# Attention and a routed mixture of experts on one core: later places for the routing, scalar row sums, and a first unit that is turned further ahead

## The chip, the cores and the metric

The kernel runs on one core of a Trainium2 chip. The metric is the device time of one execution in microseconds (us). The core has TensorE for matmuls (PE in the rows), which also loads the weights of each matmul (PEld), VectorE (DVE), ScalarE (ACT), GpSimd (POOL), SyncE (SP), which here mainly issues transfers, and 16 DMA engines. [...]

## What is computed

Attention over 8 batches and 12 heads (448 positions, head size 64), with scores capped by a tanh, and after it a mixture of experts over the 3584 tokens of 768 numbers:

```
scores = cap * tanh(scale * q @ k.T / cap);  attn = softmax(scores);  x = attn @ v
logits = x @ w_gate                          # 3584 x 8
for idx in argsort(-logits.flatten()):       # greedy, largest logit first
    tok, e = idx // 8, idx % 8
    if assigned[tok] >= 0 or counts[e] >= 448: continue
    assigned[tok] = e;  counts[e] += 1
out[mask_e] = relu(x[mask_e] @ w1[e]) @ w2[e]   # w1[e]: 768 x 1024, w2[e]: 1024 x 768
```

Each of the 8 experts takes exactly 448 tokens. The greedy assignment falls into 8 phases: in each one the first expert that becomes full is found, with the logit at which it does, and its tokens are fixed.

## The kernel before

**Attention** takes the first 350 us. At its end come the logits of the last batch. The attention output x, transposed, is turned back by TensorE (L37), scaled by POOL (L45) and written to a table `xs` in DRAM in "units"; those of the last four batches are left for the time in which the first routing runs.

**A routing phase** (class `Routing`) finds a threshold in three searches A, B and C of 5, 6 and 5 steps. A step compares all candidates with three trial values (two comparisons on VectorE, `cmpD` at L450, one on ScalarE, `cmpA`), sums the counts with a small matmul (L454, `psR<-r_cd,r_bo`), and forms the next trial values (`fl` L458, `r_HA`, `r_HB` or `r_HC` L461). Before the searches `propose` builds the candidates (L401 to L418), TensorE turns them (`flip`, L428), VectorE copies them (`VAt`, `q`, `VBCt`). After them `best` adds rows `R` by matmuls in fp32 with a matrix of ones (L509). `finalise` then marks the tokens (`gt` L530, a scan L534), adds up places with two small matmuls (L540, L541), builds one-hot tables (`oj`, `oh`, `rj`, to L555) and makes the list of 448 row numbers with 8 matmuls (L560) and one more (L567, `psR<-ev,r_sel`, called **sel** below).

**The experts.** Each expert works on its 448 tokens in fp32 that is split in two parts (h and l). Its rows are gathered from `xs` by four indirect transfers that POOL issues (L691) into one buffer `xg`, and turned chunk by chunk (6 chunks of 128 columns, 4 transposes each, `xtr`, L700). Layer 1 has 8 units of 18 matmuls (L721, tiles of 448 columns), layer 2 has 8 tiles of 24 or 16 matmuls (L748, 384 columns), 176 in all, so an expert is 320 matmuls. Weights arrive in `w1r` and `w2r`, issued by SP once the expert's number `ei` is known, early in `finalise`; ScalarE and POOL split them (L664, L668).

**What sets the order.** From the first expert on all compute engines keep the order in which the code is written. The routing of the next expert is a Python generator. `tick()` is called after each matmul of the experts and advances the generator when as many matmuls have gone by as its last `yield` said: the table `HA`, `HB` and constants such as 4, 12, 18. So the place of a phase in the matmuls is the sum of its yields, and the next phase starts as soon as one is over. The chunks of the next expert are turned at fixed places, the first one behind matmul 260 of an expert. The gather is issued behind `sel`. The first routing has no expert to run beside; its order is written by hand for TensorE and ScalarE, with the units of x put between the counts (`UN`), and VectorE's is left to a scheduler.

## Time and profile before

| | |
|---|---|
| median of 3 runs | 959.45 us (958.63 to 960.04) |
| the profiled execution | 957.35 us, of it 955.6 us from its first to its last instruction |
| PE busy | 898.8 us (94%) |
| DVE, ACT, POOL busy | 582.9, 576.1, 348.7 us |
| mean granted clock | 0.98 |

The profiled execution lies 2.1 us below the median of the runs. Its stages by the trace: attention to about 350 us, the first routing and the first gather to about 412 us (the "seam"), the experts to 948 us, then the last rows on their way out. A time is read as microseconds from the first instruction. A row of the timeline gives the start and the length of a run of like instructions on one engine, and in brackets how long the engine sat idle before it and what ended that.

### The profile page before, as it was taken

How to read it: one execution, taken by the hardware profiler on the slowest of the kernel's cores; microseconds unless marked ns; L12 is line 12 of the kernel's file. 1: busy time of each engine (PE TensorE's matmuls, PEld its weight loads, DVE VectorE, ACT ScalarE, POOL GpSimd, SP SyncE). 2: the span in 40 equal slices, each digit the busy share in tenths (PEclk: the TensorE clock that was granted, in tenths of full speed). 3: DMA queues.
4: the chain of work that ended last, by engine and by line, in shares of the span. 5: the costliest groups of instructions: out<-in, count | busy, mean ns of one | idle time of the engine just before them, and what ended most of it. 6: DMA issues, size and time to landing. Idle time of an engine off the chain costs nothing.

```text
span 955.6 us, 16304 instructions
## 1 busy us (share of the span) xinstructions
PE 898.8 (94%) x5742; PEld 617.0 (65%) x5742; DVE 582.9 (61%) x1956; ACT 576.1 (60%) x795; POOL 348.7 (36%) x474
## 2 busy tenths in 40 slices
PE   5899999999999977599999999999999999999996
PEld 1223333333322325378889889889889889899996
DVE  3779797988879767666665556556556556211210
ACT  6999899999999937264372372462561651432520
POOL 5100000000000007473484483393492672682831
PEclk9999999999999997699999999999999999999999
DMA  9799988778872025741632624615416407551301
GB/s 128 106 139 132 172 129 163 107 149 153 167 155 47 1 116 167 242 147 37 237 108 86 226 70 126 214 42 190 160 31 223 148 11 239 182 182 51 107 9 50
DMA packets 290803, 123.01 MB, mean 129 GB/s; under 512 B 224768, under 2 KB 275712, under 8 KB 290208
## 3 DMA queue, kind: packets, MB, share of 16 engines
q1 hardware_dynamic: 282960, 91.45, 43.1%
q0 software_dynamic: 5904, 30.28, 9.0%
q8 instruction: 45, 0.74, 0.3%
q10 hardware_dynamic: 1856, 0.23, 0.2%
q14 instruction: 38, 0.31, 0.1%
HBM read 97.15 MB, written 24.77 MB: 128 GB/s over the span
## 4 chain that ended last, share of the span: by engine, by line
PE 39%; issue 6%; DMA 6%; POOL 5%; DVE 1%; ACT 0%; POOLq 0%
PE psH L721 21%; PE psH L748 15%; DMA xg<-xs,idx 6%; POOL xg L691 2%; PE psX L700 2%; POOL out_dram L733 1%; POOL w1l L668 1%; PE psR L560 1%; POOL w2l L668 1%; DVE cmpD L450 0%; PE psR L509 0%; DVE hh L728 0%; ACT hh L726 0%; PE psR L454 0%; POOL gap L666 0%
## 5 line engine op out<-in xcount | busy, mean ns | idle before, releaser
L748 PE MATMUL psH<-w2h,hh 128*128 128x384 f32 x896 | 249.2, 344 | 0.0
L748 PE MATMUL psH<-w2l,hh 128*128 128x384 f32 x512 | 175.0, 342 | 0.0
L150 ACT ACTIVATE e<-psS,s 128x896 f32<-128x896 f32 x168 | 161.1, 1001 | 20.4 <-PE psS L144 10.6
L748 PEld LDWEIGHTS psH<-w2h,hh 128*128 128x128 f32 x896 | 163.0, 189 | 0.3
L154 ACT ACTIVATE e<-e,bias,capt 128x1792 f32<-128x1792 f32 (+2 forms) x74 | 154.4, 2087 | 2.5
L721 PE MATMUL psH<-xgh,w1l 128*128 128x448 f32 x384 | 142.1, 370 | 1.5 <-POOL gap L666 1.5
L721 PE MATMUL psH<-xgl,w1h 128*128 128x448 f32 x384 | 142.7, 372 | 0.2 <-DVE xgl L703 0.2
L721 PE MATMUL psH<-xgh,w1h 128*128 128x448 f32 x384 | 142.7, 372 | 0.0
L144 PE MATMUL psS<-tq,tk 64*64 64x448 f32 x1152 | 127.4, 556 | 10.2 <-DVE rcap L229 6.7
L668 POOL TENSOR_TENSOR w1l<-w1r,w1h 128x768 fp32r<-128x768 f32 x62 | 114.2, 1841 | 30.7 <-ACT w1h L664 24.9
L668 POOL TENSOR_TENSOR w2l<-w2r,w2h 128x768 fp32r<-128x768 f32 x64 | 118.1, 1845 | 16.6 <-ACT w2h L664 12.6
L172 PE MATMUL psA<-e,nv 128*64 128x448 f32 x576 | 124.1, 552 | 0.0
L754 ACT ACTIVATE on<-psH 128x384 f32<-128x384 f32 x48 | 23.7, 493 | 134.2 <-PE psH L748 113.7
L728 DVE SCALAR_TENSOR_TENSOR hh<-psH,hh 128x64 fp32r<-128x64 f32 (+1 forms) x128 | 44.1, 386 | 97.0 <-ACT hh L726 90.6
L158 DVE TENSOR_TENSOR es<-es,e 128x896 f32<-128x896 f32 (+1 forms) x94 | 102.0, 1085 | 1.9
L748 PEld LDWEIGHTS psH<-w2l,hh 128*128 128x128 f32 x512 | 96.7, 189 | 0.0
L144 PEld LDWEIGHTS psS<-tq,tk 64*64 64x64 f32 x1152 | 36.8, 133 | 81.9 <-issue 50.9
L172 PEld LDWEIGHTS psA<-e,nv 128*64 128x64 f32 x576 | 34.9, 136 | 83.8 <-issue 70.8
L721 PEld LDWEIGHTS psH<-xgh,w1l 128*128 128x128 f32 x384 | 72.6, 189 | 7.3 <-POOL gap L666 1.9
L721 PEld LDWEIGHTS psH<-xgl,w1h 128*128 128x128 f32 x384 | 72.7, 189 | 6.1 <-DVE xgl L703 1.3
L721 PEld LDWEIGHTS psH<-xgh,w1h 128*128 128x128 f32 x384 | 72.7, 189 | 5.3 <-ACT xgh L702 0.6
L733 POOL DMA_INDIRECT out_dram<-on,idx x31 | 30.4, 981 | 118.4 <-PE psX L700 47.1
(246 smaller groups left out, 1209.2 us busy)
## 6 DMA issues: line engine op xcount, KB each, us to landing
w1r<-in_moe_w_dram SPq DMA_DIRECT2D x64, 384.0 KB
w2r<-in_moe_w_dram SPq DMA_DIRECT2D x32, 768.0 KB
k<-in_k_dram SPq DMA_DIRECT2D x92, 112.0 KB
q<-in_q_dram SPq DMA_DIRECT2D x92, 112.0 KB
nv<-in_v_dram SPq DMA_DIRECT2D x72, 128.0 KB
xs<-xn POOLq DMA_DIRECT2D x4, 1344.0 KB
xs<-xn SPq DMA_DIRECT2D x4, 896.0 KB
xd<-xT POOLq DMA_DIRECT2D x2, 1344.0 KB
```

What stands on the lines that cost most here:

```text
L144: for c in range(2): nc.tensor.matmul(ps[c*64:c*64+64,h,:S],tks[g,0][hp,o,u*128+c*64:u*128+c*64+64],tks[g,1][hp,o,:],start=True,stop=True)
L150: nc.scalar.activation(ev(g,r),ps[:,:,:S],AF.Tanh,scale=s1)
L154: nc.scalar.activation(e,e,AF.Exp,scale=capt,bias=bias)
L158: t=es_t[g]; add=lambda o,a,b: nc.vector.tensor_tensor(o,a,b,op=ALU.add)
L172: nc.tensor.matmul(avp[g,o][h*64:h*64+64,:S],z[:,j,HG*h+o,:],ev(g,3*o+j)[:,h,:],start=(j==0),stop=(o==1 and j==2 and op is None))
L668: (eng or nc.gpsimd).tensor_tensor(view(l),r,view(h).bitcast(F32),op=ALU.subtract)
L691: g=nc.gpsimd.indirect_dma_start(out=t[:n,j*DM:(j+1)*DM],out_offset=None,in_=xs,in_offset=bass.IndirectOffsetOnAxis(ap=res[p][0][:n,j:j+1] ...
L721: nc.tensor.matmul(ps[:,:C],a[:,c,:],b[:,c,:],start=(m==0),stop=(m==DC*3-1)); m+=1
L728: nc.vector.scalar_tensor_tensor(h[:,d:d+b-a],ps[:,a:b],0.0,h[:,a:b].bitcast(F32),op0=ALU.max,op1=ALU.subtract)
L733: st=nc.gpsimd.indirect_dma_start(out=dst,out_offset=bass.IndirectOffsetOnAxis(ap=ix,axis=0),in_=src,in_offset=None)
L748: nc.tensor.matmul(ps[:,:HD],h[:,f,a:a+128],spl[p,2,hf,f//2][w][:,f%2,:],start=(m==0),stop=(m==nm-1))
L754: if t<3: nc.scalar.activation(ons[p][0][:,t*DM+hf*HD:t*DM+hf*HD+HD],ps[:,:HD],AF.Copy)
```

## The change

- **Places.** The yields of a search step go from 6 and 11 (phase 1, phases from 2) to 7 and 10, and with the 3 of `HB` from 9 and 14 matmuls per step to 10 and 13. The first unit starts the generator after 18 matmuls and not 6. For phases from 2 on, `finalise` waits for matmul 145 of the expert, so for the second layer.
- **Sums.** The three rows of `best` are first added as scalars (128x1) on VectorE, so `best` has one matmul where it had two.
- **Proposals.** `propose` is cut in two: for phase 1 and the last four chunks of the logits the second half (VB, VC, K1, K2) runs behind the first comparisons.
- **Seam.** VectorE's order is now written by hand, too. Ten small matmuls on the identity stand ahead of the turn of VA, others around the matmuls of `finalise`, in place of 16 matmuls of 512 columns on `oh`.
- **First unit.** Four chunks of the first expert are turned ahead of its first matmul, two of them into buffers of the matmul results, the others inside the unit. The weight loads that wait for the gather now wait for its last piece in `xg` and not for its row numbers. The split of the second layer's weights starts one unit later for the first expert.

```
-        HA=[6,11]; HB=3
+        HA=[7,10]; HB=3
...
-                s.propose(L,0,s.NC)
+                (s.propose_a if p==1 else s.propose)(L,0,s.NC)
                 yield 30
             yield from (s.search(wp,turned if p==0 else ()) if p<s.E-1 else s.last(wp))
-            yield 4
+            yield -((p-1)*320+145) if p>1 else 4
             yield from s.finalise(wp,L,p<s.E-1)
...
-        hint[0]=next(gen,0)
+        h=next(gen,0)
+        hint[0]=max(-h-now[0],4) if h<0 else h
...
+        def total(a,b):
+            t=wp.tile([128,1],F32,name="tot",bufs=4); jk=wp.tile([128,1],F32,name="jk",bufs=2)
+            v.tensor_scalar(jk,a,b,None,op0=ALU.add,op1=ALU.add,accum_out=t)
+            return t
+        def row(a,b):
+            th=total(a,b)
             r=wp.tile([128,8],F32,name="R",bufs=6); jk=wp.tile([128,1],F32,name="jk",bufs=2)
             v.tensor_scalar(r,s.e8,th,None,op0=ALU.mult,op1=ALU.add,accum_out=jk)
...
-        yield from s.select(wp,s.V["q"],"B",[lambda: row(tA)])
+        yield from s.select(wp,s.V["q"],"B",[lambda: keep.append(total(tA,s.zero))])
...
-        mid=[lambda: row(tB)]
+        mid=[lambda: row(keep[0],tB)]
...
-        for n,r in enumerate(((s.R[0],s.R[1]),(s.R[-1],s.e8k))[a]): nc.tensor.matmul(ps[:112,0:8],s.onesf,r,start=n==0,stop=n==1)
+        nc.tensor.matmul(ps[:112,0:8],s.onesf,s.R[a],start=True,stop=True)
...
-    N0=1; UN=[2,1,2,1,0,2,2,1,2,2,0,2,2,2,2,0]
+    N0=1; UN=[1,2,1,2,0,2,2,1,2,2,0,2,2,2,0,0]
...
-    with tc.manual_schedule(engines={ET.PE,ET.Activation}):
+    with tc.manual_schedule(engines={ET.PE,ET.Activation,ET.DVE}):
...
+            for _ in range(n): nc.tensor.matmul(wu[0][:,:128],ident,ident,start=True,stop=True)
...
-        if gate: nc.gpsimd.tensor_copy(t[0:1,0,0:1],res[p][0][0:1,0:1])
+        if gate is not None: nc.gpsimd.tensor_copy(t[0:1,0,0:1],gate)
...
+        seq=[(c,k) for c in range(DC) for k in range(3)]
+        if p==0 and f==0:
+            seq=[(0,0),(0,2)]
+            for c in range(1,DC): seq+=[(c,0),(c,2),(c-1,1)]
+            seq+=[(DC-1,1)]
...
+            if p==0 and f==0 and k==1 and c<2: xtr(0,c+4)
...
-    for _ in range(16): nc.tensor.matmul(wu[:112],rt.id16,rt.oh.rearrange("p r c -> p (r c)")[:,:512],start=True,stop=True)
...
-    hint[0]=6
-    for c in range(2): xtr(0,c)
+    hint[0]=18
+    for c in range(4): xtr(0,c,ph if c>1 else None)
```

Three places of TensorE's order show what moves. The line numbers behind a plus or in "now" are those of the changed kernel, where L560, L567, L700, L721, L748 and L428 have become L577, L585, L725, L751, L778 and L435.

First the end of the first routing: `oh` and `rj` are the tables, L771 the matmuls on `oh` that fill the pause. Before, around sel:

```order
L560 LDWEIGHTS oh
L560 MATMUL psR<-rj,oh 128x56
L771 LDWEIGHTS r_id_268
L771 MATMUL psX<-oh,r_id_268 112x512
L771 LDWEIGHTS r_id_268
L771 MATMUL psX<-oh,r_id_268 112x512
L771 LDWEIGHTS r_id_268
L771 MATMUL psX<-oh,r_id_268 112x512
L567 LDWEIGHTS r_sel
L567 MATMUL psR<-ev,r_sel 128x14
```

and now:

```order
L577 LDWEIGHTS oh
L577 MATMUL psR<-rj,oh 128x56
L648 MATMUL psX<-ident 128x128 x3
L585 LDWEIGHTS r_sel
L585 MATMUL psR<-ev,r_sel 128x14
L648 MATMUL psX<-ident 128x128 x22
```

The three matmuls of 512 columns ahead of sel have become three of 128 columns; two more of 512 stood ahead of the eight L560 matmuls, and stand there no longer.

Then the first unit of the first expert. Before:

```order
L700 MATMUL psX<-ident,xg 128x128 x8
L721 MATMUL psH<-xgh,w1h 128x448
L721 MATMUL psH<-xgl,w1h 128x448
L721 MATMUL psH<-xgh,w1l 128x448
L700 MATMUL psX<-ident,xg 128x128 x4
L721 MATMUL psH<-xgh,w1h 128x448
L721 MATMUL psH<-xgl,w1h 128x448
L721 MATMUL psH<-xgh,w1l 128x448
L700 MATMUL psX<-ident,xg 128x128 x4
```

and now:

```order
L725 MATMUL psX<-ident,xg 128x128 x8
L725 MATMUL psH<-ident,xg 128x128 x8
L751 MATMUL psH<-xgh,w1h 128x448
L751 MATMUL psH<-xgh,w1l 128x448
L751 MATMUL psH<-xgh,w1h 128x448
L751 MATMUL psH<-xgh,w1l 128x448
L751 MATMUL psH<-xgl,w1h 128x448
L725 MATMUL psX<-ident,xg 128x128 x4
```

Sixteen transposes, not eight, stand ahead of the first matmul, and the matmul that needs the second part `xgl` of a chunk comes three or four places behind the chunk's first.

Last the place in the first expert where the first chunk of the second expert is turned (L700, now L725, behind matmul 260). Before:

```order
L428 LDWEIGHTS r_VC
L428 MATMUL psV<-r_id_268,r_VC 128x112
L748 MATMUL psH<-w2h,hh 128x384 x2
L748 MATMUL psH<-w2l,hh 128x384
L748 MATMUL psH<-w2h,hh 128x384
L700 MATMUL psX<-ident,xg 128x128 x4
```

and now:

```order
L778 MATMUL psH<-w2h,hh 128x384
L725 MATMUL psX<-ident,xg 128x128 x4
L778 MATMUL psH<-w2h,hh 128x384
L778 MATMUL psH<-w2l,hh 128x384
L778 MATMUL psH<-w2h,hh 128x384 x2
L778 MATMUL psH<-w2l,hh 128x384
L778 MATMUL psH<-w2h,hh 128x384 x2
L778 MATMUL psH<-w2l,hh 128x384
L435 LDWEIGHTS r_VA
L435 MATMUL psR<-r_id_270,r_VA 128x112
```

The routing has moved back against the transposes: the next phase's turns of VA and VC stood ahead of them and now VA's come behind. Counted over the whole order, sel stands behind matmul 200, 199, 198, 197, 196, 195 of experts 0 to 5 before (that of the last expert's list behind 277 of expert 5), and now behind 228, 211, 194 and, from expert 3 on, 179, that of the last list behind 179 of expert 6. The transposes of the next expert stay behind matmuls 260, 284, 292, 300, 308 and 316.

## Rows read from the trace of the kernel before

**Rows 1.** Busy time by stretch: length, busy us (instructions) per engine, clock, DMA.

```profile
355.00:372.00 17.00, 12.25 (x59) 10.09 (x60) 11.97 (x81) 11.33 (x30) 10.62 (x11) 0.50 0.48 173
399.60:406.00 6.40, 4.64 (x16) 3.23 (x17) 3.67 (x10) 1.82 (x3) 0.83 (x1) 0.50 0.95 302
410.00:956.00 546.00, 526.20 (x2967) 482.93 (x2965) 259.43 (x1293) 234.61 (x485) 295.84 (x323) 1.00 0.38 123
```

**Rows 2.** Waits of TensorE, whole run: us in total, times, longest.

```profile
PE psR L454 <- DVE cmpD L450: 10.5, 12, 2.0
PE psX L700 <- DMA xg<-xs,idx: 7.0, 11, 1.6
PE psH L721 <- POOL gap L666: 1.5, 1, 1.5
```

**Rows 3.** Timeline of TensorE at the gather for expert 1.

```profile
454.77 0.18 PE L567 MATMUL psR<-ev,r_sel 128*128 128x14 f16 x1
...
465.82 0.38 PE L700 MATMUL psX<-ident,xg 128*128 128x128 f32 x2
...
467.86 0.42 PE L748 MATMUL psH<-w2h,hh 128*128 128x384 f32 x1
```

**Rows 4.** Stretches of the first chunk's transposes, experts 2 to 5; last a later chunk.

```profile
602.97:604.91 1.94, 0.79 (x5) 0.36 (x4) 0.04 (x2) 0.47 (x2) 1.10 (x2) 1.00 0.44 145
671.43:673.16 1.73, 0.79 (x5) 0.36 (x4) 0.00 (x0) 0.35 (x1) 1.10 (x2) 1.00 0.10 34
739.75:741.06 1.31, 0.79 (x5) 0.36 (x4) 0.00 (x0) 0.17 (x1) 0.86 (x1) 1.00 0.07 26
807.21:809.05 1.84, 0.78 (x5) 0.36 (x4) 1.41 (x5) 0.00 (x0) 1.22 (x2) 1.00 0.08 30
541.00:541.36 0.36, 0.36 (x6) 0.36 (x4) 0.32 (x4) 0.00 (x0) 0.22 (x1) 1.00 0.40 117
```

**Rows 5.** Timeline of VectorE in search A of the first routing.

```profile
362.44 0.16 DVE L458 SCALAR_TENSOR_TENSOR fl<-psR,r_HA 128x4 f32<-128x4 f32 x1 [0.57 <-PE psR L454]
...
363.98 0.16 DVE L458 SCALAR_TENSOR_TENSOR fl<-psR,r_HA 128x4 f32<-128x4 f32 x1 [0.28 <-PE psR L454]
...
364.61 0.21 DVE L483 TENSOR_SCALAR_CACHE_REDUCE R<-r_e,th 128x8 f32<-128x8 f32 x1
```

**Rows 6.** Lines L505 and L530: ns min/median/max, first and last start.

```profile
L505 DVE SCALAR_TENSOR_TENSOR sx<-wt,wB,r_e8c x7: 226/227/806, 385.1 to 788.5; 112x8 f32<-112x8 f32 x7
L530 DVE TENSOR_SCALAR gt<-qq,wB x8: 235/238/1090, 385.8 to 803.8; 112x32 f32<-112x32 f32 x8
```

**Rows 7.** Timeline of POOL in the seam.

```profile
380.79 6.08 POOL L45 TENSOR_TENSOR xn<-raw,rin 112x512 f32<-112x512 f32 x6 [0.43 <-ACT raw L42]
391.50 0.73 POOL L685 MEMSET xg<- 64x768 f32 x1 [4.63 <-DMA xs<-xn]
```

**Rows 8.** Timeline of VectorE, end of the first routing.

```profile
389.69 0.39 DVE L555 TENSOR_TENSOR rj<-oj,r_idc 112x448 f16<-112x448 f16 x1
...
392.03 0.21 DVE L564 TENSOR_REDUCE ev<-ek 128x14 f16<-128x56 f16 x1
```

**Rows 9.** Timeline of TensorE, same stretch.

```profile
389.83 1.01 PE L771 MATMUL psX<-oh,r_id 112*112 112x512 f16 x2 [1.98 <-DVE oh L553]
390.63 1.04 PE L560 MATMUL psR<-rj,oh 112*128 112x56 f16 x8
...
392.75 0.22 PE L567 MATMUL psR<-ev,r_sel 128*128 128x14 f16 x1
```

**Rows 10.** Timeline of TensorE: first matmuls of the first and second unit.

```profile
403.50 0.74 PE L721 MATMUL psH<-xgh,w1h 128*128 128x448 f32 x1
...
411.86 0.37 PE L721 MATMUL psH<-xgh,w1h 128*128 128x448 f32 x1
```

**Rows 11.** Timeline of TensorE: the matmuls of `best` in expert 0.

```profile
446.25 0.66 PE L509 MATMUL psR<-R,r_onesf 128*112 128x8 f32 x6
...
446.96 0.61 PE L748 MATMUL psH<-w2h,hh 128*128 128x384 f32 x2
```

## What was predicted

> **What bounds the kernel now.** I read the busy time by stretch first. From 410 us to the end TensorE is at 1.00 and busy for 526.20 of 546.00 us [rows 1]; the experts are bound by TensorE, and only its gaps and extra matmuls can be saved there. Ahead of it lies the seam, in which a chain of counts runs between VectorE and TensorE, and in which TensorE is at 0.50 for two stretches [rows 1]: 17 us in which it is busy for 12.25, and 6.4 us in which the first unit begins. The waits of TensorE come next [rows 2]: the counts wait 10.5 us for comparisons (seam and phase 1 together), the transposes 7.0 us for gathered rows, and one unit 1.5 us for POOL. So there are three accounts: seam, gathers, routing's own matmuls. The timeline gives the price of each.
>
> **Gathers, where the change costs.** Sel for expert 1 starts at 454.77; its first transposes start at 465.82, 60 matmuls later, so 0.184 us per matmul with what lies between; experts resume at 467.86, when the last piece has landed [rows 3]. A gather thus needs 467.86-454.77=13.09 us from sel, and 60 matmuls cover 11.05 of them. That stretch is 2.04 us long, an undisturbed chunk 0.36 [rows 4], so 1.7 us are lost. For the gathers of experts 3 to 6 the same view gives 1.94-0.36=1.58, 1.37, 0.95 and 1.48 [rows 4].
>
> By the order, sel now stands behind matmul 228, 211, 194, then 179. The first gather loses 28 matmuls of its cover, 28*0.184=+5.15 us. The second loses 12: +2.2. The third gains 4: -0.7 of its 1.58. The next three gain 16 to 18, about 3 us, more than they lose: -(1.37+0.95+1.48)=-3.8. I leave the 13.09 as it is, since the weight loads that share the DMA engines are released with the expert's number, which moves with sel.
>
> TensorE will then sit still for some 6.8 us at 466 and for 4 at 534. Behind the gather of the seam, with a pause of the same kind, the first 6.4 us ran at 0.50 [rows 1], busy for 4.64, so half of that, 2.3, was lost. No row shows a fall among the experts, whose waits are under 2 us. For the first wait I take +1.9, near that row (from 0 to 3.2, half the 6.4 us at full use); for the second, shorter one, half of it, +1.0 (0 to 1.9).
>
> At expert 6 the gather for expert 7 now comes behind matmul 179 and no longer at the start of layer 1, ahead of the split of w1. The wait for POOL's `gap` [rows 2] has no cause left: -1.5, and with the restart -1.7.
>
> **Routing among the experts.** `best` holds TensorE from 446.25 to 446.96, 0.71 us for its four fp32 matmuls [rows 11]. Two go, in six phases: -6*0.355=-2.1. The scalar sums that replace them stand on VectorE, which is busy for 259 of the 546 us [rows 1]; without that cover each would cost about the 0.21 of `R` [rows 5]. From expert 3 on the routing rests until matmul 145, which costs nothing as long as the gather keeps its cover: 260-179=81 matmuls, 14.9 us against 13.09. The later split of w2 for expert 0 costs nothing either: its last pieces, cut in unit 7, are needed 88 matmuls into layer 2. In phase 1 steps come every 10 matmuls, which is 0.2 us more per step for a chain that is late at 9; against it, the second half of the proposal and the first unit's work are put on VectorE ahead of a count. I take +0.3, from -1.5 to +1.5: neither half of the seam's and phase 1's 10.5 us [rows 2] is separable in advance.
>
> **The seam.** Its end is set by the chain from the first comparison to the list of rows.
> (a) In search A and B three counts stand behind eight transposes at half clock, and `fl` then waits 0.57 where it else waits 0.28 [rows 5] (two such, and one of 0.69): 1.0 together. Ten matmuls now fill part of TensorE's pause ahead of VA's turn. If they keep the clock up, all of it goes; I take -0.6 (0 to -1.0).
> (b) `R` (0.21 us) stands ahead of the first comparisons of B and C [rows 5] and now behind them, where VectorE waits for the count anyway: -0.4.
> (c) `sx` and `gt` take 0.806 and 1.090 us in the seam against medians of 0.227 and 0.238 [rows 6], both at 385 us, under POOL's products, which run from 380.79 to 386.87 [rows 7]. By the table `UN` the two units behind the fifteenth step have moved ahead, so POOL should be done: -(0.58+0.85)=-1.43, from 0.
> [...]
> (d) `rj` is done at 390.08 [rows 8]; the L560 matmuls start at 390.63, behind two of 512 columns [rows 9]: -0.45. `ev` is done at 392.24 [rows 8], sel starts at 392.75 behind three more [rows 9]: -0.3, as three short ones remain.
> (e) Costs: sel's matmul of `best` waits for one more sum. No row has a sum of 128x1; the nearest, `R` of 128x8, takes 0.21 [rows 5]. Less the dropped matmul: +0.2. The second half of the last proposal moves from over VA's turn to over the first count; VectorE then waits for the longer of the two: +0.2.
> [...]
> Sum of the chain: -0.6-0.4-1.43-0.75+0.4=-2.8.
>
> **First gather and unit.** The weight loads now wait for the last gathered piece, not for the numbers: -0.2, an estimate between 0 and -1. The first unit runs from 403.50 to 411.86 [rows 10], 8.36 us. Eighteen matmuls of 448 columns at 0.184*448/384=0.21 and four chunks of transposes at 0.36 [rows 4] make 5.3; of the 3.1 over, 2.3 are the clock of [rows 1], and 0.8 are waits for `xgl` and for transposes in between. The new order spreads these and starts with eight transposes more, during which the clock can rise: -1.1 (0 to -2.2, if also half the clock's cost goes).
>
> **Sum.** +5.15+1.9+2.2+1.0-0.7-3.8-1.7 = +4.05 for the gathers; -2.1+0.3 for the routing; -2.8 for the chain; -0.2-1.1 for the first unit: -1.85. On the profiled execution's 957.35 that is 955.5; it lies 2.1 under the median of the runs, 959.45, and the forecast is on that: **957.6 us**.
>
> **Rivals.**
> *The clock stays low after the first late gather* (slower). If it needs, after 7 us of stillness, what it needed in the stretch of 17 us, in which TensorE was busy for 12.25 at 0.50 [rows 1], the loss is 6.1 and not 1.9: 957.6+4.2=961.8. It decides from about 3.8 us over my 2.9, so from 13 us of matmuls at half clock in the two places together. For it: the same clock did fall after short pauses in the seam. Against: behind a gather it lasted only 6.4 us.
> *The seam gives nothing* (the same). If the products of POOL still meet `sx` and `gt`, (c) is 0; if the gather's last piece sets when the first unit can run, and the memset of `xg`, which waits for the last units' writing to `xs` and ends at 392.23 [rows 7], sets when the gather starts, the rest of the gain goes too: 957.6+1.43+1.3=960.3, within 0.2% of before. For it: that memset ends under 2 us ahead of the list. Against: the units end sooner now.
> *The seam gives more* (faster). The ten matmuls hold the clock, so all of (a); the first unit saves 2.2, phase 1 0.5 and the first late gather ends at full clock: 957.6-0.4-1.1-0.8-1.9=953.4.
> *The late gathers do not bite* (the change does less than its order says). If a gather that starts later meets fewer loads and lands 5 us sooner after sel, the +5.15, +2.2, +2.9 go: 957.6-10.25=947.3. For it: 13.09 us is long against the 403.50-392.75=10.75 us from sel to the first matmul in the seam [rows 9, 10]. Against: the stretches of the later gathers [rows 4] stay between 1.3 and 1.9 us, with other loads beside each (DMA share 0.07 to 0.44).
>
> **Chances and range.** Forecast 0.42 (its own range 955.5 to 960), clock stays low 0.15, seam nothing 0.20, seam more 0.18, no bite 0.05. About 1.9 us, 0.2%, is what a measurement of this kernel can tell from no change. The forecast lies at that edge, so half of its 0.42 is faster and half the same; with the two fast rivals that makes 0.44 faster, 0.41 the same, 0.15 slower. The range leaves out the last rival and the ends of the next two: 951.5 to 962.5.
>
> **What would show it.** Right: TensorE waits for `xg` twice, near 467 for 6 to 7 us and near 535 for 4, and a granted clock of 0.50 for some us behind at least the first; no such wait from expert 3 on, nor one for `gap`; the list's sel in the seam near 390 and not 392.75; `sx` and `gt` near their medians in the seam; the second unit's first matmul near 407.5 and not 411.86. Wrong: a gather that lands within 10 us of sel, a clock of 1.00 behind the waits, or a first unit that still takes 8 us. What would spoil the sum most is the price of the first late gather, the largest term on either side, since nothing of before shows a gather that late.

## The result: 0.3% slower

The changed kernel takes 961.91 us (median of 18 runs, 960.0 to 963.92), the kernel before 958.56 (18 runs, 957.44 to 960.7): a ratio of 1.0034, with a 95% interval of 1.0026 to 1.0041. That is 3.3 us more, where 1.85 less was forecast. More runs put the median of before 0.9 us under the one the forecast was made on; its time of 957.6 would be 956.7 on the new base. The range held the time, the sign was wrong.

The two profiled executions lie 5.7 us apart (963.07 and 957.35), 2.4 more than the medians. Part of this is the seam, whose end moves by about 1 us from one execution to the next: four kernels of this study that have the gather and the first unit of before (sums_alone, sums_padded, sums_in_place, places_alone) reach the first expert matmul at 404.3 to 404.9 us, the kernel before in its profile at 403.5. One issue of the first gather on POOL makes 0.9 us of that: it took 1.18 us in the profile of before and 2.05 to 2.07 in those four.

A ledger by stages, from the starts of instructions in the two timelines, shows where the 5.7 us lie:

| stage | before, us | after, us | difference |
|---|---|---|---|
| up to VA's turn | 354.22 | 353.78 | -0.4 |
| VA's turn to the last count of the first routing | 29.16 | 33.00 | +3.8 |
| last count to sel | 9.37 | 7.76 | -1.6 |
| sel to the first expert matmul | 10.75 | 13.34 | +2.6 |
| first unit | 8.36 | 5.03 | -3.3 |
| second unit to layer 2 of expert 0 | 30.44 | 32.43 | +2.0 |
| layer 2 of expert 0 (gather for expert 1) | 38.78 | 45.84 | +7.1 |
| expert 1 (gather for expert 2) | 68.66 | 71.42 | +2.8 |
| experts 2 to 5 | 273.17 | 265.57 | -7.6 |
| experts 6 and 7, to the last matmul | 124.20 | 124.67 | +0.5 |

The waits of TensorE over the whole run (us in total, times, longest) answer to [rows 2]; the wait for POOL's `gap` is gone, the one for gathered rows has grown from 7.0 to 11.0:

```profile
PE psR L461 <- DVE cmpD L457: 11.7, 11, 2.7
PE psX L725 <- DMA xg<-xs,idx: 11.0, 10, 2.1
```

TensorE's timeline at the gather for expert 1 answers to [rows 3]:

```profile
462.71 0.18 PE L585 MATMUL psR<-ev,r_sel 128*128 128x14 f16 x1
...
470.70 0.33 PE L725 MATMUL psX<-ident,xg 128*128 128x128 f32 x1 [2.15 <-DMA xg<-xs,idx]
...
475.37 0.67 PE L778 MATMUL psH<-w2h,hh 128*128 128x384 f32 x1
```

The experts resume 475.37-462.71=12.66 us behind sel (13.09 before), and 32 matmuls cover 5.84 of it (470.70 less the 2.15 of idle time, from sel). The matmuls that follow are slow: 0.67 against 0.42 in [rows 3]. The busy time by stretch (length, busy us of each engine, clock, DMA), for the two low stretches of the first routing and behind the two late gathers, answers to [rows 1]:

```profile
357.60:364.40 6.80, 4.96 (x24) 4.15 (x25) 5.16 (x38) 4.64 (x13) 4.05 (x4) 0.50 0.46 147
...
367.80:398.50 30.70, 22.90 (x113) 20.16 (x112) 20.71 (x120) 15.64 (x37) 18.77 (x18) 0.50 0.61 182
...
475.40:480.60 5.20, 5.20 (x19) 4.89 (x20) 1.84 (x6) 1.88 (x4) 1.82 (x1) 0.51 0.08 26
...
548.70:552.10 3.40, 3.40 (x16) 3.40 (x16) 1.30 (x9) 1.33 (x3) 1.29 (x1) 0.50 0.02 5
```

TensorE stands still, then works 5.2 us at a granted clock of 0.51, where 1.00 is full speed. About half of them, 2.6, is lost, an estimate from that clock; the 384-column matmuls start every 0.32 us there, and behind the same gather before every 0.17. Behind the second late gather the clock is low, 0.50, for 3.4 us, from 1.2 us after the experts resume (547.48). In the first routing it is low, 0.50, for 6.8 and for 30.7 us, where it was for 17 [rows 1] and for 10.2:

```profile
385.70:395.90 10.20, 6.33 (x24) 3.68 (x24) 6.97 (x29) 0.86 (x2) 3.73 (x5) 0.50 0.91 258
```

This, too, changes from one execution to the next: p1_whole, which leaves the first routing as the change has it, is low there for 13.7 and 17.0 us.

The row that was not expected is in VectorE's timeline. The second half of phase 1's proposal stands behind the first two comparisons:

```profile
412.93 1.47 DVE L418 TENSOR_SCALAR r_b<-r_u 112x32 int32<-112x32 int32 x1
...
414.65 1.95 DVE L420 TENSOR_TENSOR r_VB<-r_P,r_Bt 112x256 f16<-112x256 f16 x1
```

POOL at the same time, and the count that waits:

```profile
412.49 1.85 POOL L693 TENSOR_TENSOR w1l<-w1r,w1h 128x768 fp32r<-128x768 f32 x1 [6.86 <-issue]
414.27 0.09 POOL L691 MEMSET gap<- 1x1 f32 x1
414.47 1.85 POOL L693 TENSOR_TENSOR w1l<-w1r,w1h 128x768 fp32r<-128x768 f32 x1
```

```profile
419.30 0.19 PE L461 MATMUL psR<-r_cd,r_bo 128*128 128x4 bf16 x1 [2.65 <-DVE cmpD L457]
```

One op ends at 414.40, POOL's split at 414.34; the next long one at 416.60, POOL's next split at 416.32. An op is called held below if it is longer than its like elsewhere and ends thus, at the end of what POOL runs or shortly behind it. Right behind the wait of 2.65 us the clock falls as well:

```profile
419.00:422.40 3.40, 3.10 (x9) 2.80 (x10) 2.06 (x12) 3.23 (x8) 2.31 (x3) 0.50 0.89 229
```

By line (count: ns min/median/max) these ops in the changed kernel and, second fence, in the kernel before:

```profile
L418 DVE TENSOR_SCALAR r_b<-r_u x15: 160/166/1473, 95.2 to 806.2; 112x4 int32<-112x4 int32 x8, 112x32 int32<-112x32 int32 x7
...
L420 DVE TENSOR_TENSOR r_VB<-r_P,r_Bt x15: 192/424/1952, 95.6 to 806.6; 112x32 f16<-112x32 f16 x8, 112x256 f16<-112x256 f16 x7
...
L457 DVE TENSOR_SCALAR_CACHE_REDUCE cmpD<-r_qt,th x63: 426/442/446, 367.7 to 785.5; 128x224 bf16<-128x224 f16 x63
```

```profile
L411 DVE TENSOR_SCALAR r_b<-r_u x15: 160/165/178, 95.6 to 800.9; 112x4 int32<-112x4 int32 x8, 112x32 int32<-112x32 int32 x7
...
L413 DVE TENSOR_TENSOR r_VB<-r_P,r_Bt x15: 191/194/428, 96.0 to 801.3; 112x32 f16<-112x32 f16 x8, 112x256 f16<-112x256 f16 x7
```

Before, no op of the proposal was ever held: none began while POOL ran a split or a product. The comparisons never are held, though 139 of the 224 in the changed kernel began while POOL ran one (447 ns at most). So there are ops on VectorE that wait for POOL and ops that don't, and the change moved the eight ops of the second half from where POOL was quiet to where it is busy; two of them were held in phase 1.

In the seam the same happens to the second half of the last proposal. VectorE, and POOL's two products beside it:

```profile
355.70 0.92 DVE L420 TENSOR_TENSOR r_VB<-r_P,r_Bt 112x32 f16<-112x32 f16 x1
...
356.73 0.90 DVE L422 TENSOR_SCALAR r_Ct<-r_c 112x4 f16<-112x4 int32 x1
```

```profile
355.51 2.09 POOL L45 TENSOR_TENSOR xn<-raw,rin 112x512 f32<-112x512 f32 x2 [3.38 <-ACT raw L42]
```

The two ops end at 356.62 and 357.63, the second just behind POOL's two products (357.60).

### The profile page after: what moved, and what is told of

Its sections match the earlier page's. It is cut to its first block, busy times and chain, and to the rows that moved or that the text cites. A ratio compares the mean times of both kernels' runs of the same rounds, so it can differ in the third digit from the quotient of the medians.

```text
span 961.3 us, 16399 instructions
## 1 busy us (share of the span) xinstructions
PE 907.7 (94%) x5776; PEld 631.6 (66%) x5776; DVE 589.7 (61%) x1984; ACT 575.5 (60%) x795; POOL 349.0 (36%) x475
## 4 chain that ended last, share of the span: by engine, by line
PE 76%; issue 8%; ACT 4%; POOL 4%; DVE 4%; DMA 3%; ACTq 0%; POOLq 0%; DVEq 0%
PE psH L751 21%; PE psH L778 19%; PE psA L172 11%; PE psS L144 10%; PE psM L191 3%; DMA xg<-xs,idx 3%; ACT e L150 3%; PE psS L149 2%; PE psX L725 2%; PE psA L179 2%; PE psL L37 2%; POOL xg L716 1%; PE psM L37 1%; ACT e L154 1%; DVE cmpD L457 1%
## 5 line engine op out<-in xcount | busy, mean ns | idle before, releaser
L778 PE MATMUL psH<-w2h,hh 128*128 128x384 f32 x896 | 252.4, 347 | 0.0
L778 PE MATMUL psH<-w2l,hh 128*128 128x384 f32 x512 | 176.4, 345 | 0.0
L778 PEld LDWEIGHTS psH<-w2h,hh 128*128 128x128 f32 x896 | 165.7, 192 | 0.2
L751 PE MATMUL psH<-xgh,w1h 128*128 128x448 f32 x384 | 143.5, 374 | 0.0
L751 PE MATMUL psH<-xgh,w1l 128*128 128x448 f32 x384 | 143.3, 373 | 0.0
L751 PE MATMUL psH<-xgl,w1h 128*128 128x448 f32 x384 | 142.5, 372 | 0.0
L693 POOL TENSOR_TENSOR w2l<-w2r,w2h 128x768 fp32r<-128x768 f32 x64 | 117.9, 1842 | 17.0 <-ACT w2h L689 13.3
L778 PEld LDWEIGHTS psH<-w2l,hh 128*128 128x128 f32 x512 | 98.0, 191 | 0.0
L751 PEld LDWEIGHTS psH<-xgh,w1h 128*128 128x128 f32 x384 | 73.2, 191 | 5.4
L751 PEld LDWEIGHTS psH<-xgh,w1l 128*128 128x128 f32 x384 | 73.1, 190 | 5.5
L751 PEld LDWEIGHTS psH<-xgl,w1h 128*128 128x128 f32 x384 | 72.9, 190 | 5.4
L756 ACT ACTIVATE hh<-psH 128x448 fp32r<-128x448 f32 x64 | 34.8, 543 | 67.1 <-PE psH L751 62.7
```

Of the source, the lines that this page charges most:

```text
L693: (eng or nc.gpsimd).tensor_tensor(view(l),r,view(h).bitcast(F32),op=ALU.subtract)
L751: nc.tensor.matmul(ps[:,:C],a[:,c,:],b[:,c,:],start=(m==0),stop=(m==DC*3-1)); m+=1
L756: nc.scalar.activation(h[:,:C],ps[:,:C],AF.Relu)
L778: nc.tensor.matmul(ps[:,:HD],h[:,f,a:a+128],spl[p,2,hf,f//2][w][:,f%2,:],start=(m==0),stop=(m==nm-1))
```

## Experiments

**Theory A**: the second half of the two proposals (phase 1, and the last chunks in the seam) is slow where it now stands, since VectorE waits there for POOL's running instruction, and this spoils a gain that is otherwise about as forecast. **Rivals**: the late places cost it all (the gathers, or the count's place in the first unit); the low clock lengthens the seam whatever the proposals do. The kernels of the experiments were timed in 4 to 12 runs each beside the kernel before on the same chip; the chip was not the same for all, so two of them are compared by their ratios to before, and microseconds of a difference come from these:

| kernel | median, us | ratio to before, 95% interval |
|---|---|---|
| changed kernel | 961.91 | 1.0034, 1.0026 to 1.0041 |
| p1_whole | 957.63 | 0.9996, 0.9987 to 1.0005 |
| seam_whole | 959.27 | 1.0016, 1.0006 to 1.0025 |
| late_quiet | 960.59 | 1.0019, 1.0010 to 1.0028 |
| places_alone | 962.55 | 1.0047, 1.0034 to 1.0059 |
| unit_alone | 957.50 | 0.9987, 0.9978 to 0.9996 |
| sums_alone | 959.19 | 1.0008, 0.9999 to 1.0017 |
| sums_padded | 959.37 | 1.0009, 0.9998 to 1.0020 |
| sums_in_place | 958.12 | 0.9993, 0.9984 to 1.0002 |
| early_whole | 945.51 | 0.9868, 0.9853 to 0.9882 |
| turn_later | 946.02 | 0.9872, 0.9857 to 0.9887 |
| issue_free | 945.18 | 0.9855, 0.9836 to 0.9873 |
| combined | 940.08 | 0.9812, 0.9796 to 0.9828 |
| combined_issue | 939.43 | 0.9801, 0.9785 to 0.9816 |
| combined_in_place | 938.28 | 0.9785, 0.9766 to 0.9803 |
| without_ten | 939.75 | 0.9795, 0.9775 to 0.9814 |

**p1_whole**, on the changed kernel:

```
-            if post and i==(2 if s.cur==1 else 0): post()
+            if post and i==0: post()
...
-            if s.cur==1: late=[lambda: s.propose_b(0,s.NC)]
...
-                (s.propose_a if p==1 else s.propose)(L,0,s.NC)
+                s.propose(L,0,s.NC)
```

> The changed kernel with the whole proposal of phase 1 ahead of its first comparisons, as before. Theory A (the second half of the proposal is slow because it now stands beside POOL's split of w1, and the first count waits for it): the wait of 2.65 us at the count near 419 goes or falls under 0.7, two ops that took 1.47 and 1.95 us fall to about 0.2 and 0.4, and the time is 2 to 2.5 us under the changed kernel, so about 1 us over the kernel before. Rival B (the first count of phase 1 is late because of its new place in the matmuls): the wait stays near 2.6 and the time with it, 3.4 us over before.

0.38% of the time goes, 3.6 us, more than theory A's 2.5; the wait of 2.65 us at that count is 0.24, and from its first matmul to layer 2 expert 0 takes 33.35 us and not 37.46. Rival B is out. The stretch in the changed kernel and, second fence, in p1_whole shows what the extra is:

```profile
407.88:445.34 37.46, 34.41 (x170) 28.97 (x169) 25.67 (x124) 22.65 (x49) 26.02 (x27) 0.94 0.40 130
```

```profile
406.69:440.04 33.35, 32.74 (x170) 27.50 (x169) 21.42 (x116) 22.67 (x49) 26.06 (x27) 1.00 0.45 145
```

TensorE stands still for 0.61 us and not 3.05, so 2.4 less, and the 3.4 us at a clock of 0.50 behind the wait, worth up to 1.7 as an estimate from that clock, are gone. What the turns of VB and VC add, which also go back to the first count, is not separated.

**seam_whole**, on the changed kernel:

```
-            first=late[0]; late[0]=lambda: (s.propose_b(s.NC-4,s.NC),first())
...
-            (r.propose if b<7 else r.propose_a)(L1,4*b,4*b+4)
+            r.propose(L1,4*b,4*b+4)
```

> The changed kernel with the whole proposal of the last four chunks ahead of VA's turn, as before; the ten matmuls on the identity stay. Theory A: the two ops of 0.92 and 0.90 us beside POOL's products go, the first two counts stand 1.9 and not 2.7 us apart, TensorE's pause of 2.2 us ahead of VB's turn goes, and the time is 0.8 to 1.5 us under the changed kernel, more if the clock then falls for a shorter time. Rival C (the seam is longer only because the clock is low for longer, whatever the proposal does): less than 0.4 us.

0.18% goes, 1.7 us. The first two counts stand at 356.37 and 357.90, 1.53 apart and not 2.67, and sel at 390.78 and not 394.54. Rival C falls as the cause of the whole; but the clock may take part: the fifteen steps from the first count to the sixteenth take 26.65 us, 1.78 each and not 1.53, and the granted clock from 358 to 386 us is between 0.53 and 1.00 in stretches of 4 us. That it makes them slower is not shown. A single trace can't price the seam: from the first count to the sixteenth it is 30.05 us in the changed kernel and 28.13 in p1_whole, which has the same seam, and 26.65 here. The price taken is that of the medians.

**late_quiet** leaves all of the change and moves POOL's split only:

```
+    split1(0,2)
     hint[0]=18
...
-            if f+2<FC: work[17 if p==0 and f==0 else 3]=[lambda: split1(p,f+2)]
+            if f+2<FC and (p or f): work[17 if p==0 and f==0 else 3]=[lambda: split1(p,f+2)]
```

> The changed kernel, all of it, but POOL's split of the third w1 piece is written ahead of the first transposes, while POOL waits for the gather, and not behind the first unit's 17th matmul. So the second half of phase 1's proposal keeps its late place, and POOL is quiet there at first. Theory A (VectorE's ops wait for POOL's running instruction): the op of 1.47 us falls to about 0.2, at most one op still waits for the next split, the wait of 2.65 us at the second count falls under 1, and the time is 1.5 to 2.5 us under the changed kernel. Rival E (eight full-width ops ahead of the second count are too many, POOL or not): the wait stays over 2 us and the time within 0.7 of the changed kernel.

VectorE's timeline has the same ops at the same place, POOL quiet up to 414.68:

```profile
413.11 0.17 DVE L418 TENSOR_SCALAR r_b<-r_u 112x32 int32<-112x32 int32 x1
...
413.54 0.42 DVE L420 TENSOR_TENSOR r_VB<-r_P,r_Bt 112x256 f16<-112x256 f16 x1
...
414.75 1.84 DVE L425 SCALAR_TENSOR_TENSOR r_K<-r_kk,r_Ct 112x32 f32<-112x32 f16 x1
```

```profile
414.68 1.85 POOL L693 TENSOR_TENSOR w1l<-w1r,w1h 128x768 fp32r<-128x768 f32 x1 [6.97 <-ACT w1h L689]
```

The two long ops are back to 0.17 and 0.42. The last op of the eight, 0.18 us long in other phases, starts 0.07 after POOL's next split and ends with it. That shows what theory A says: same place, same ops, and the length follows POOL. Rival E falls by the wait, 1.43 us and not over 2. The time falls by 0.15%, 1.4 us, a little under what theory A expected, and the two intervals overlap slightly; one op is still caught, and the count waits more than the 1 us that was expected.

**places_alone**, on the kernel before: `HA=[7,10]`, the lock to matmul 145 and `hint[0]=18` from the change, nothing else.

> The kernel before with the new places alone: 10 and 13 matmuls per step, the lock to matmul 145, the generator's start after 18. The account of the gathers by the trace of the changed kernel: +5.2 and +3.1 us for the first two, with the low clock behind them, -0.9, -1.3, -0.9 and -1.5 for the next four, -1.3 for POOL's wait: about +2.4, and with fewer stalls in phase 1 some +1.5 to +2.5 us over before. Rival D (all of the loss lies in the seam, and the places pay for themselves): no more than +0.5.

0.47%, 4.5 us, more than expected. From the first transposes' place to the next matmul the gathers for experts 1 and 2 take 7.84 and 4.28 us (2.05 and 2.18 before), and from there to the end of the expert 15.5 and 14.9 us, where before had 13.2 and 13.3. The expectation had left out the wait of the first gather's first piece. Against that, from the second unit to layer 2 expert 0 takes 28.64 us and not 30.44. Rival D is out: by themselves the places lose. Whether they lose more than the whole change the intervals don't tell.

**unit_alone**, on the kernel before: the new order of the first unit, its four chunks ahead, the gate on the last gathered piece and the later split of w2.

> The kernel before with the first unit's new order alone: four chunks turned ahead of its first matmul, the weight loads gated by the gather's last piece, the later split of w2; sel and all places as before. By the two traces the first unit takes 5.0 us from its first matmul and not 8.4, and what lies between the rows' landing and that matmul grows by 0.9: -2.4, so about 956. If it was the higher clock from the longer run of small matmuls that made the unit short and not its order: -1 or less.

0.13% goes, 1.2 us, half of what was expected, and near the -1.3 of the prediction; it lies between the theory and its rival and doesn't decide between order and clock. The first matmul comes 2.23 us later and layer 2 only 0.22 later.

**sums_alone**, on the kernel before: `total`, `row` and the single matmul of `best` from the change.

> The kernel before with the scalar sums alone, so one matmul in best where there were two. By the prediction's price, 0.355 us for each of six routings among the experts: -2.1, and about 0 in the seam: 956 to 957. If VectorE's longer chain ahead of best eats it, within 0.5 of before.

Nothing is gained (0.08% more, the interval holds 0). From layer 2 to the first transposes experts 1 to 4 each take 0.35 to 0.4 us less, as priced. But layer 1 takes 0.2 more in each of them, and 0.57 in expert 7, in which no routing runs. Layer 1 of expert 7 (start, end; 145 or 146 matmuls), in the changed kernel, in sums_alone and in sums_in_place:

```profile
892.42:922.17 29.75, 29.75 (x146) 27.04 (x146) 6.00 (x16) 14.60 (x23) 27.00 (x31) 1.00 0.16 47
```

```profile
888.53:918.28 29.75, 29.75 (x145) 27.04 (x145) 6.00 (x16) 14.61 (x23) 27.05 (x31) 1.00 0.16 48
```

```profile
887.36:916.54 29.18, 29.18 (x145) 27.05 (x145) 6.00 (x16) 14.61 (x23) 27.05 (x31) 1.00 0.16 49
```

At one clock the same 144 matmuls take 0.2066 us each or 0.2027.

**sums_padded**, the same with wider small tiles (`[128,4]` for k8s and zero, `[128,8]` for tot).

> The kernel before with the scalar sums alone, as in the run of the sums alone, but the new small tiles are as wide as what they replace: k8s and zero 16 bytes each where e8k had 32, tot 32 bytes per buffer and not 4. In the run of the sums alone each matmul of layer 1 in expert 7 took 0.2066 us and not 0.2027, and those of experts 1 to 5 0.2038 and not 0.2022. Theory F (the small tiles shift what lies behind them in memory, and an operand of layer 1 then starts in a worse place): the pitch goes back to 0.2027 and the time to 956.5, 2 us under before. Rival G (the pitch comes from something else in the routing): pitch and time stay, 959.

The same time and pitch, 0.2066 us. By the author's count from the code this edit leaves the operands of layer 1 where they are in sums_alone, so that it would not part theory from rival; the 160 bytes of the next expectation are from that count, too. No trace shows an address.

**sums_in_place** is meant to put them back (its edit against sums_alone):

```
-        s.k8s=t("k8s",[128,1])
+        kz=t("kz",[128,8]); s.k8s=kz[:,0:1]
...
-        s.zero=t("zero",[128,1]); nc.gpsimd.memset(s.zero,0.0)
+        s.zero=kz[:,1:2]; nc.gpsimd.memset(s.zero,0.0)
...
-            r=wp.tile([128,8],F32,name="R",bufs=6); jk=wp.tile([128,1],F32,name="jk",bufs=2)
+            r=wp.tile([128,8],F32,name="R",bufs=2); jk=wp.tile([128,1],F32,name="jk",bufs=2)
```

> The kernel before with the scalar sums alone, and with two buffers of R and not six and the small constants in one tile, so that weights, tokens and results lie at the addresses of the kernel before (in the run of the sums alone 160 bytes further). Theory F (the place of the layer-1 operands sets the pitch): 0.2027 us per matmul in expert 7, and the time falls by the 0.36 us per routing that best shows: 956.7, 2 us under before. Rival G (the pitch comes from another part of the sums): 0.2066 and about 959.

The pitch is 0.2027 again, and layer 1 of experts 1 to 5 takes what it took before. That is the pitch that theory F expected: what differs from sums_alone is the number of `R`'s buffers and the tile of the two constants, and no routing uses them in expert 7. That the place of the operands makes the pitch is the author's reading, and which operand it is stays open. The 2 us that were expected don't come: the time is 0.07% under before, and its interval still holds 0: from the first expert matmul on, its profiled execution is 1.0 us faster than before, although layer 1 of expert 0 is 0.8 slower; the seam ended 1.1 later.

**early_whole**, on the changed kernel: both proposals whole, `HA=[6,10]`, `hint[0]=6`, so sel behind 200 and 183.

> The changed kernel with both proposals whole and with phase 1 as early as before (9 matmuls per step, start after 6; phases from 2 on keep 13 and the lock), so sel for the first two experts' gathers stands behind matmul 200 and 183. By the account of the gathers, +5.2 and +3.1 go and -1.7 and the half of 2.2 come: 8 us less for the gathers; with the proposals 11 us under the changed kernel, less 1 for the stalls of phase 1 at 9 matmuls per step: 950 to 953. If the low clock and not the wait is what costs, the same; if the gather has a fixed place in time, not 13 us from sel, no more than 5 us under the changed kernel.

945.51, 1.32% under before and 4.5 us under the expected range. The waits for gathered rows fall from 11.0 to 3.1 us in total:

```profile
PE psX L723 <- DMA xg<-xs,idx: 3.1, 4, 1.9
```

Layer 2 of expert 0 takes 37.5 us and not 45.8, expert 1 66.7 and not 71.4, so 13.0 us for two gathers; the expectation had 8. It left out the first piece's own wait, 2.15 in the timeline above; both gathers also lose less than before (1.11 and 0.35 us from the transposes' place to the next matmul, 2.05 and 2.18 before).

**turn_later**, on the changed kernel: both proposals whole, sel where the change put it, but the chunks of the next expert at 284 to 320 for two experts:

```
-    CP=[[int(y) for y in x] for x in ',,,,,0,123,45'.split(',')]
+    CP=[[int(y) for y in x] for x in ',,,,,0,123,45'.split(',')]; CL=[[int(y) for y in x] for x in ',,,,,,012,34'.split(',')]
...
+            if p<2 and u==7: wk={16:[lambda: xtr(p+1,5)]}
+            ffn2(p,u%4,u//4,(CL if p<2 else CP)[u],wk)
```

> The changed kernel with both proposals whole, with sel where the change put it (behind 228 and 211), and for the first two experts with the next expert's chunks turned behind matmuls 284, 292, 300, 308, 316 and 320 and not 260 to 316. If the gathers cost what their cover lacks, 56 matmuls or 10.3 us stand against 12.7 us for the first, 73 or 13.4 us for the second: about 2.4 us lost at the first, at most 1 behind it for the clock, nothing at the second. Phase 1 at 10 matmuls per step takes 3.9 us less in expert 0 than at 9 in the kernel with early phases. So 942 to 945, against 945.5 for that one. If the gather's end moves with the place of the transposes, or if the chunks turned so late hold up the next expert's first unit: 947 or more.

946.02, a little over. The gather for expert 1 then costs 1.24 us, the next nothing. Two ways to give a gather its 13 us, an earlier sel or later transposes, give times within each other's interval.

**issue_free**, on early_whole: VectorE's two splits of w1 behind the proposal.

> The kernel with whole proposals and early phase 1, with VectorE's two splits of w1 behind the proposal and no longer beside the gather's issues. In all kernels of this study in which such a split starts about 0.25 us into POOL's second issue that issue takes 2.05 us, else 1.2. Theory H (the issue waits for VectorE's instruction): the second issue takes about 1.2, the last piece lands 0.9 us sooner, and the time is 0.5 to 1 us under 945.5. Rival (the second issue is slow by its place, or the transfers set the landing): no change.

POOL's second gather issue in the changed kernel, VectorE's split beside it, and then the issue in issue_free:

```profile
396.96 2.07 POOL L716 DMA_INDIRECT xg<-xs,idx  x1 [0.30 <-issue]
```

```profile
397.21 0.95 DVE L693 TENSOR_TENSOR w1l<-w1r,w1h 128x768 fp32r<-128x768 f32 x1
```

```profile
393.05 1.20 POOL L714 DMA_INDIRECT xg<-xs,idx  x1 [0.30 <-issue]
```

Theory H is borne out on the instruction, which takes 0.9 us less without the split beside it. Over the kernels of this study the second issue took 2.05 to 2.07 us in all twelve in which a split began 0.25 us into it, and 1.19 to 1.20 in the four without one. But the kernel before has the split, 0.30 us into the issue, and the issue took 1.18; so it is not every such split, and what decides is not shown. From sel to the first expert matmul it takes 12.32 us and not the 13.09 of early_whole. The time moves by 0.13%, within both intervals.

**combined**, on the changed kernel: whole proposals, `hint[0]=6` with 10 and 13 matmuls per step, later transposes for three experts, and the padded tiles.

> The changed kernel with whole proposals, the generator's start after 6, so sel behind 216, 199 and 182 for the first three gathers, the chunks of the next expert turned from matmul 284 on in the first three experts, and the padded small tiles. 68 matmuls or 12.4 us stand against 12.7 for the first gather, so nothing is lost at any gather but 0.3: 1.3 us under the kernel that turns later, 0.5 more at the third gather, and 1.1 more if theory F holds: 943. If the chunks turned at 316 and 320 hold up the next expert, 945 or more.

940.08, 3 us better than expected. Nothing is lost at any gather among the experts. 1.6 of the 3 us are expert 0's layer 1, 32.74 us against 34.38 in turn_later: TensorE stands still for 0.26 us and not 0.64, and the mean clock is 1.00 and not 0.97, as the low stretch that ends the seam reaches 2.3 us into the layer in turn_later. So most of it is the clock of one execution. **combined_issue** adds issue_free's edit:

> The same with VectorE's splits of w1 behind the proposal. By theory H 0.5 to 1 us under the combined kernel: 942 to 942.5; by its rival the same time.

939.43, in the expected direction, within the intervals. Last the tiles put back (**combined_in_place**) and, on that, no ten matmuls ahead of VA's turn (**without_ten**):

> The combined kernel with VectorE's splits behind the proposal, and with the tiles at the addresses of the kernel before. By theory F 0.57 us less in each of experts 6 and 7 and some 0.1 to 0.2 in each other one: 1.5 to 2 us under 939.4. By rival G the same time.

> The same kernel without the ten matmuls on the identity ahead of VA's turn. If they hold up the clock, it falls at 355 as in the kernel before and not near 359, three counts then wait 0.3 to 0.4 us longer for transposes, and the run takes 0.6 to 1 us more. If they hold nothing up, within 0.3 us.

combined_in_place has the lowest median, 938.28, 2.15% under before, and layer 1 of experts 6 and 7 takes 29.19 us each and not 29.75, as theory F expected; its time is 0.16% under combined_issue, within both intervals. without_ten takes 0.1% more, which is inside its interval and at the upper end of what was expected if the ten hold up the clock; but its chain of counts is no slower (16 counts from 356.27 to 382.94, against 356.27 to 383.12 in combined_issue and 356.66 to 385.24 in combined_in_place). So the ten matmuls show no gain, and none is ruled out.

## Why the prediction was wrong

**The step that failed** is the price of the proposals' second halves. The prediction gave them +0.2 in the seam ((e): "moves from over VA's turn to over the first count; VectorE then waits for the longer of the two") and put them, net of what the later steps gain, in the +0.3 of phase 1. It moved them with the durations that they had where POOL was quiet. They measured +1.7 us in the seam (seam_whole) and +3.6 in phase 1 (p1_whole): VectorE's ops are held beside POOL (in phase 1 1.47 and 1.95 us for 0.17 and 0.42), the count waits (2.65 us), and behind the wait the clock is at 0.50 for 3.4 us. The new steps of phase 1 gained 1.8 by themselves (places_alone, second unit to layer 2), so phase 1 came to about +1.8 net.

The two runs make 5.3 together. No run has both halves back and nothing else; turn_later has both, and of the 1.62%, 15.5 us, by which it is under the changed kernel, its two gathers take 11.3 by the traces, which leaves 4.2. Without this cost the changed kernel would stand at 956.6 to 957.7, by either number under the 958.56 of before: the sign was decided there. The prediction had the reading in hand: in (c) it read that `sx` and `gt` are stretched under POOL's products [rows 6, 7] and gained by freeing them. It did not ask which ops the change puts under POOL's work. In these traces a VectorE op of this kind has no duration of its own; it has one for each neighbour, as `r_VB` with 0.42 us and, beside a split, 1.95.

**Gathers: right.** Forecast +4.05 for gathers and POOL's wait. By the stretches from the first transposes' place to the next matmul, and what follows at low clock, expert 1's gather cost 4.8 more and an estimated 2.6 for the clock (forecast 5.15 and 1.9), expert 2's 1.3 and 1.8 (2.2 and 1.0), the next four saved 1.0, 1.3, 0.9 and 1.5 (0.7 and 3.8 together), POOL's wait 1.3 (1.7; 1.9 in places_alone, where layer 1 of expert 6 doesn't have the slower pitch): +4.5. That places_alone as a whole is also +4.5 us is in part chance, as it holds the gain of phase 1's steps, too. The fixed 13 us from sel held: 12.66 and 12.28. The clock was under-sized: 5.2 us at 0.51 behind the first gather and 3.4 at 0.50 behind the second, 4.4 us lost together, an estimate from these clocks, where 2.9 were in the sum.

**Routing's matmuls: right in price, wrong in sum.** A removed matmul of `best` is worth 0.35 to 0.4, as priced. A cost that no step had took most of it back in sums_alone, and 0.56 us in each of experts 6 and 7 of the changed kernel: with the new small tiles each layer-1 matmul took 4 ns more where no routing runs (0.2066 us and 0.2027).

**Seam: half right.** From the last count to sel the chain gained 1.6 (forecast for (c), (d) and the sums of (e): -2.0); kernels with the seam of before range from 8.5 to 9.4 us there, the changed kernel has 7.8. `sx` and `gt` were no longer held in the seam, where they had taken 0.806 and 1.090 us; by line (ns min/median/max) they answer to [rows 6]:

```profile
L520 DVE SCALAR_TENSOR_TENSOR sx<-wt,wB,r_e8c x7: 226/227/227, 388.7 to 790.4; 112x8 f32<-112x8 f32 x7
```

```profile
L545 DVE TENSOR_SCALAR gt<-qq,wB x8: 231/234/238, 388.9 to 859.3; 112x32 f32<-112x32 f32 x8
```

Terms (a) and (b) are not to be seen: the clock fell a little later (at 357.6 us and not 355.0) and was at 0.50 for longer (37.5 us of the first routing and not 27.2), and a step behind `r_qt` took 2.58 us and not 1.94, as `r_qt`, an op with two inputs, took 1.13 beside POOL and not 0.50. In seam_whole, sel is 1.97 us earlier than before, against -2.8. The sum of 128x1 in (e), for which no row was at hand, took the 0.21 us of `R` that stood in for it (`jk` at 387.21 us).

The traces part VectorE's ops in two. Held were `r_VB`, `r_K`, `r_qt` and `sx`, which read two tensors (by 1.5, 1.7, 0.6 and 0.6 us), and `r_b`, `r_Ct` and `gt`, plain TENSOR_SCALARs that read one (by 1.3, 0.7 and 0.85 us); the comparisons, which read one and add up an accumulator, never were (447 ns at most). So the number of tensors that are read does not part them, and what does no run shows.

**First unit: right with the gate's and POOL's part.** It took 5.0 us and not 8.4, but began later: the second and the fourth issue of the gather took 2.07 and 1.99 us, each beside a split on VectorE, where the profile that the forecast was made on has 1.18 and 0.93. unit_alone shows -1.2 for all of it, where -1.3 was forecast.

**Rivals.** None came as written. "The seam gives nothing" named the right place and the right neighbour, POOL, but the wrong ops. "The clock stays low" was too dark: 5.2 us behind the first late gather, not the 12.25 taken from the seam.

**What stays open.** What the later turns of VB and VC have in the 3.6 us of p1_whole; what the hand-written order of VectorE, the small matmuls around `finalise` and the new `UN` are worth, which no run has by themselves; why the clock in the seam falls and rises where it does from one execution to the next; and why a layer-1 matmul takes 4 ns more in experts 6 and 7 of the changed kernel, but under 1 ns more in its experts 1 to 5.

## What to carry to other kernels

Ask of each op that is moved not only how long it took but who ran beside it: before an op is put under another engine's work, look at the longest of its kind there, not at the median. A transfer with a nearly fixed time from its trigger, 12.2 to 13.7 us here where a gather was waited for, is best counted in the matmuls that cover it, and either end may be moved; behind a stretch of 6.8 us without full work TensorE ran at 0.51 for 5.2 us here, an estimated 2.6 more. And when small tiles change, compare a stretch in which nothing else changed: a pitch that differed by 2% at a granted clock of 1.00 (0.2066 us and 0.2027) pointed here to the tiles, since it came back with two buffers of `R` and one tile for the constants.

## What the runs showed that was not expected

- Some VectorE ops that start while POOL runs a split end with it or up to 0.3 us later: 0.18 us became 1.84, 0.42 became 1.95, 0.17 became 1.47. Comparisons with a single f16 input were never held (426 to 446 ns for the 63 of one line above).
- It works the other way, too: POOL's gather issue went from 1.2 to 2.07 us when a split of 0.95 us on VectorE began 0.25 us into it. In the kernel before such a split began 0.30 into it, and the issue took 1.18.
- Layer-1 matmuls of 448 columns in expert 7 took 0.2066 us in sums_alone and sums_padded and 0.2027 in sums_in_place, which has other small tiles and the same work; in the kernel before they took 0.2027, too.
